# First batch of an FFT convolution, with the products laid out by (frequency of the pair, k2), ahead of a gated MLP in fp32 on one Trainium2 core

## The chip, the core and the metric

One core of one Trainium2 chip runs the whole program. The metric is the device time of one execution in microseconds (us), the median of several runs. A profiled execution has its own time, and its trace covers a span that is a little shorter than that time. The engines are named as in the profile: PE (TensorE, matmuls), PEld (its weight loads), DVE (VectorE), ACT (ScalarE), POOL (GpSimd) and SP (SyncE, which here only issues DMAs).

## What is computed

Two steps follow each other, all in fp32. The first is a long causal convolution, done by FFT, of `u = x * v` with a filter that a small MLP makes from `pos_emb`; its result is multiplied by `x`. The second is an MLP with a SiLU on 24,960 tokens.

```python
B, S, D = 2, 12480, 128
h_filt = (np.maximum(pos_emb @ w1, 0.0) @ w2) * np.exp(-0.01 * pos)[:, None]
Uf = np.fft.rfft(x * v, n=2 * S, axis=1)
Hf = np.fft.rfft(h_filt, n=2 * S, axis=0)
y = np.fft.irfft(Uf * Hf[None], n=2 * S, axis=1)[:, :S]
tok = (x * y).reshape(B * S, D)
h = tok @ moe_w_in                                # 128 -> 2048
out = (h / (1.0 + np.exp(-h))) @ moe_w_out        # 2048 -> 128
```

## The kernel before

The transform length is split as 2 x 98 x 64. The 98 outer frequencies are handled in 49 pairs (`NQ`), each of 2 outer frequencies `k` with 64 inner frequencies `k2`, real and imaginary parts `c` side by side. The program has three stages.

**Stage A** (to about 110 us) makes the filter's first transform `Xh` and the first transform `X` of batch 0.

**The products of batch 0** (about 110 to 284 us) are one loop, `for it in range(-1, NQ)`, with the steps of several pairs interleaved by hand. Every engine works through its own queue in the order in which the code issues. The steps are:

- `load_fb` loads a table `fb` of 256 KB for a pair, which holds its forward matrix (`[:, :, 0]`) and its inverse one (`[:, :, 1]`). It is issued on ACT's queue for pair `it + 4`; the buffers are seven deep.
- `pair_u` (L470, tile `up`): two matmuls of 128 x 128 with 256 columns give the pair's spectrum, with (c, k2) on the partitions. `times_i` (L487, L489, tile `uw`) copies it on ACT, halves of 64 partitions swapped and one negated.
- `hb_step` (L308, tile `hp`, copied to `zt` by ACT at L316): two matmuls of 128 x 128 with 128 columns, the filter's transform for pair `it + 3`.
- `spectrum` (L327, tile `sp`): 16 matmuls of 64 x 64 with 128 columns for pair `it + 1`. Eight of them are there because both halves of the partitions, c = 0 and c = 1, need the same filter values. Two ACT copies (L329) of 128 x 512 make `hab`, of which the lower 64 partitions are stored to `hs` for batch 1.
- `pair_p` (L495 and L502): `up` times `hab` on DVE (tile `at`), `uw` times `hab` on POOL (tile `bt`), each with one product of 512 and one of 256 elements per partition. `pair_s` (L508) adds `at` and `bt` on DVE, 768 elements, both in SBUF. `pair_v` (L512) adds the last 256 of them into the first part, on POOL (on DVE for the last two pairs).
- `last_w` for pair `it - 2`: `pair_w` (L470, tile `wp`, two buffers in two banks of PSUM), two matmuls of 128 x 128 with 256 columns, then `even_odd`: one ACT copy (L525), a sum and a difference on DVE (L527, L528), and two stores on SP's queue (L531) into `wd` in rows of 512 bytes, 64 partitions each. `ws` has two buffers.
- `side_steps` adds, from pair 25 on, loads of the MLP's weights, eight casts on ACT (L547), eight subtractions on DVE (L551, `wil`), loads of the second batch, and two products on POOL (L269, `spare`).

A string of letters, `seq3`, then orders what lies between this loop and the third stage; `s`, `v`, `u` and `U` in it stand for the sum, the last addition and the last two `last_w` of batch 0.

**The MLP** (from about 298 us to the end) runs over spans of 512 tokens, with the whole of batch 1's convolution threaded between its matmuls. `load_tile` (L647) reads `wd` back for `attn_tile` (L666). Batch 1 reads `hs` (`load_h`, L783) and `fb`, and uses `pair_p` and `even_odd` too.

PSUM has eight banks; the loop uses two each for `hp`, `sp`, `up` and `wp`.

Of the kernel before, what the change touches and what calls it, by code (L numbers as in the profile page):

```python
# [22 lines left out]
NB = 2  # L23
D = 128
# [41 lines left out]
def moe_tiles():  # L66
# [23 lines left out]
    seq3='smAvumULASahhllhhllaxxrrrrYLxhhllhhll',  # L90
# [4 lines left out]
def kernel(  # L95
# [16 lines left out]
    fb: bass.AP,  # L112
    win: bass.AP,
# [13 lines left out]
    hs = dram.tile([NQ, 64, 1024], F32, name="hs")  # L127
    wd = [dram.tile([2, NQ, 2, NI, C, D], F32, name=f"wd{b}") for b in range(NB)]
# [164 lines left out]
    def load_fb(rp, q, bufs, e):  # L293
        t = rp.tile([128, 2, 2, 128], F32, name=f"fb{q}", tag="fb", bufs=bufs)
        e.dma_start(out=t, in_=fb[q])
        return t
# [3 lines left out]
    def hb_step(q):  # L300

        if php is None:
            hp = psa.tile([128, 4, 256], F32, name=f"hp{q}", tag="ap", bufs=4)[:, 0]
            hp = hp.rearrange("p (k c n) -> p k c n", k=2, c=2)
        else:
            hp = php.tile([128, 2, 2, 64], F32, name=f"hp{q}", tag="hp", bufs=2)
        for k in range(2):
            nc.tensor.matmul(  # L308
                hp[:, k].rearrange("p c k -> p (c k)"),
                Xh[2 * q >= KA][:, 2 * q - (2 * q >= KA) * KA + k],  # L310
                fbs[q][:, k, 0],
                start=True,
                stop=True,
            )
        zs[q] = rpa.tile([128, 2, 2, 64], F32, name=f"zt{q}", tag="zt", bufs=3)
        nc.scalar.copy(out=zs[q], in_=hp)  # L316

    def spectrum(q, hab):

        zt = zs.pop(q)  # L320
        sp = [pps.tile([128, 2, 2, D], F32, name=f"sp{q}_{s}", tag=f"sp{s}", bufs=1) for s in range(2)]
        for k in range(2):
            for m in range(2):
                for s in range(2):
                    r = slice(64 * s, 64 * s + 64)
                    for h in range(0, 128, 64):
                        nc.tensor.matmul(sp[s][h : h + 64, m, k], zt[r, k, m], w2_sb[r], start=True, stop=True)  # L327
        for s in range(2):
            nc.scalar.copy(out=hab[:, :, s], in_=sp[s])  # L329
# [80 lines left out]
    for t in P["seq"]:  # L410
# [18 lines left out]
        elif t == "Z":  # L429
            begin(zq, zeros_block(n_z))  # L430
            n_z += 1
        elif t == "z":
            end(zq, False)
        elif t == "y":
            zw.append(zq[0])
            end(zq, True)
        elif t == "Y":
            end(zw)
        elif t == "H":
            begin(hq_, filter_group(n_h))  # L440
            n_h += 1
        elif t in "hg":
            end(hq_, t == "h")
        elif t in w_steps:
            next(w_steps[t], None)
        elif t == "|":
            early.release()
            xpool = pool("xpool")
            X = xpool.tile([128, R, NI * D], F32, name="X")
            rpa = pool("rp2a")  # L450
        elif t == "f":
            fbs[n_f] = load_fb(rpa, n_f, 7, nc.sync)
            n_f += 1
        elif t == "B":
            hb_step(len(zs))
# [36 lines left out]
    def pair_p(b, q, rp, u, hab, m, tag, nb, e):  # L492
# [5 lines left out]
            in1=hab[:, m, 0].unsqueeze(2).broadcast_to([128, 2, NI, D]),  # L498
# [4 lines left out]
            out=t[:, 2].rearrange("p (k d) -> p k d", k=2), in0=u[:, :, 0], in1=hab[:, m, 1], op=ALU.mult  # L503
# [17 lines left out]
    def even_odd(b, q, rp, wp, nb):  # L521

        p, tag, n = (rp, "ws", nb["ws"]) if b or q < NQ - 2 else (rpa, "fb", 7)
        ws = p.tile([128, 2, NI, D], F32, name=f"ws{b}_{q}", tag=tag, bufs=n)
        nc.scalar.copy(out=ws[:, 1], in_=wp[:, 1])  # L525
        yield ws
        nc.vector.tensor_tensor(out=ws[:, 0], in0=wp[:, 0], in1=ws[:, 1], op=ALU.add)  # L527
        nc.vector.tensor_tensor(out=ws[:, 1], in0=wp[:, 0], in1=ws[:, 1], op=ALU.subtract)  # L528
        yield ws
        for c in range(2):  # L530
            nc.sync.dma_start(  # L531
                out=wd[b][c, q].rearrange("e i t d -> t (e i) d"),
                in_=ws[64 * c : 64 * c + 64].rearrange("p e i d -> p (e i) d"),
            )
# [57 lines left out]
    nb = dict(up=2, uw=2, at=3, bt=2, wp=2, ws=2)  # L592

    def last_w(q):
        for _ in even_odd(0, q, rp, pair_w(0, q, pp, [(fbs.pop(q)[:, :, 1], prods.pop(q)[0])], nb), nb):
            pass

    for it in range(-1, NQ):
        if P.get("cut") and it == 4:
            for p in (rp, rpa, xpool, xha_pool, xhb_pool, const, pps, pp, php, dram):  # L600
                p.release()
            return
        if it + 4 < NQ:
            fbs[it + 4] = load_fb(rpa, it + 4, 7, nc.sync if it < 0 else nc.scalar)
        q = it
        if 0 <= q < NQ:
            up = pair_u(0, q, pp, [(fbs[q][:, :, 0], X[:, 2 * q : 2 * q + 2])], nb)
            _, uw = times_i(0, q, rp, up, nb)
        q = it - 1
        if 0 <= q < NQ:  # L610
            pair_s(*prods[q])
        q = it + 1
        if 0 <= q < NQ:
            hab = rp.tile([128, 2, 2, 2, D], F32, name=f"hab{q}", tag="hab", bufs=3)
            spectrum(q, hab)
            habs[q] = hab
        q = it + 3
        if 3 <= q < NQ:
            hb_step(q)
        q = it  # L620
        if 0 <= q < NQ:
            hab = habs.pop(q)
            _, at = pair_p(0, q, rp, up, hab, 0, "at", nb, nc.vector)
            _, bt = pair_p(0, q, rp, uw, hab, 1, "bt", nb, nc.gpsimd)
            prods[q] = at, bt
            nc.sync.dma_start(out=hs[q], in_=hab[0:64].rearrange("p m s k d -> p (m s k d)"))
        q = it - 1
        if 0 <= q < NQ:
            pair_v(prods[q][0], nc.vector if q >= NQ - 2 else nc.gpsimd)
        q = it - 2  # L630
        if 0 <= q < NQ:
            last_w(q)
# [10 lines left out]
    def load_tile(n):  # L643
        b, i, t2, m = tiles[n]
        w = sum(tile_widths(i, m))
        wt = slot(4096, 2 * 5 * D)[0:R].rearrange("p (c n) -> p c n", c=2)
        nc.sync.dma_start(  # L647
            out=wt[:, :, 0 : m * D],
            in_=wd[b][:, :, :, i, t2 : t2 + m].rearrange("c q e t d -> (c q) e (t d)"),
# [5 lines left out]
    def attn_tile(n, wt, xs, psp, tag):  # L655
# [5 lines left out]
        for t in range(m):  # L661
            for e in range(2):
                k = (ws[t] + 1 - e) // 2
                a = o + NQ * e
                for h in range(0, D, 64):
                    nc.tensor.matmul(  # L666
                        yp[h : h + 64, a : a + k],
                        wt[:, e, t * D + h : t * D + h + 64],
# [27 lines left out]
    for t in P["seq3"]:  # L696
# [7 lines left out]
        elif t == "s":  # L704
            pair_s(*prods[NQ - 1])
        elif t == "v":
            pair_v(prods[NQ - 1][0], nc.vector)
        elif t == "u":
            last_w(NQ - 2)
        elif t == "U":  # L710
            last_w(NQ - 1)
# [53 lines left out]
    def batch1_steps():  # L765
# [11 lines left out]
        def load_f(q):  # L777
            return load_fb(rp, q, 2, nc.sync)

        def load_h(q):  # L780
            hab = rp.tile([128, 2, 2, 2, D], F32, name=f"habr{q}", tag="hab", bufs=1)
            for h in range(2):
                nc.sync.dma_start(  # L783
                    out=hab[64 * h : 64 * h + 64].rearrange("p m s k d -> p (m s k d)"),
                    in_=hs[q],
# [179 lines left out]
def _constants():  # L965
# [14 lines left out]
    feo = np.stack([feo[:, 0::2], feo[:, 1::2]], axis=1)  # L980
    th = 2.0 * np.pi * ((k1[:, None, None] + 0.5) / N + k2[None, None, :] / C) * t2[None, :, None]
# [4 lines left out]
    fwd[1::2, C:] *= -1.0  # L986
    fb = np.stack([fwd, inv], axis=1).reshape(NQ, 2, 2, 128, 128).transpose(0, 3, 1, 2, 4)
# [4 lines left out]
    return {k: np.ascontiguousarray(a, dtype=np.float32) for k, a in dict(fa=fa, fs=fs, feo=feo, fe=fe, fb=fb, win=win).items()}  # L992
# [56 lines left out]
```

## Time and profile before

| | us |
|---|---|
| median of 3 runs | 1565.91 (1564.54 to 1567.79) |
| the profiled execution | 1563.66 |
| its span in the trace | 1561.9 |
| first product of batch 0 on DVE | at 113.13 |
| the same product of pair 48, the last one | at 278.94 |
| first matmul of the MLP | at 298.12 |

The profiled execution lies 2.25 us under the median, and the span 1.8 us under its execution. Over the whole span PE is busy 98%, DVE 80%, ACT 66% and POOL 41%; in the stretch of the products all four are busier than that, which the shares for the whole do not show.

To read the timeline below: each row has the start in us from the span's start, the duration in us, the engine, the line of the code, the operation, what it writes and reads, the shapes, and how many instructions were merged into the row. Brackets give the idle time of the engine just before it, and what ended it. A matmul in fp32 appears as two records, so "x4" is two matmuls. Ends of matmuls are modelled, and the start of the next row tells more than a row's duration.

### The profile page before, as it was taken

The page shows a single profiled execution, that of the slowest core. Times are in us where ns is not written, and L with a number is a line of the kernel's source. Part 1 is how long each engine was busy: PE and PEld are TensorE (multiplying, and loading weights), DVE is VectorE, ACT ScalarE, POOL GpSimd, SP SyncE. Part 2 cuts the span into 40 slices and gives each one's busy share as a digit, 9 for nine tenths or more (in the row PEclk, how much of TensorE's full clock was granted, in tenths as well). Part 3 has the DMA queues.
Part 4 walks back from the last instruction along what each step waited for, and adds up shares of the span by engine and source line. Part 5 has one row for each costly group of instructions (what it writes and reads, how often), then busy time and mean ns, then how long its engine had stood idle before and what let it go on. Part 6 is the DMA issues. An engine that isn't in the chain of part 4 may idle for free.

```text
span 1561.9 us, 32021 instructions
## 1 busy us (share of the span) xinstructions
PE 1529.9 (98%) x11928; PEld 1273.7 (82%) x11928; DVE 1242.8 (80%) x2091; ACT 1036.4 (66%) x1959; POOL 638.4 (41%) x669
## 2 busy tenths in 40 slices
PE   8989999799999999999999999999999999999999
PEld 8978877587788888888888888888888888888887
DVE  7558888667799999999999897777777777777776
ACT  2558887577777877877887775555555555555555
POOL 3658789422278887878788740000000000000000
PEclk9999999699999999999999999999999999999999
DMA  7667988745355555555555631111101211111100
GB/s 238 204 208 216 237 254 238 225 160 163 99 139 146 136 138 142 135 151 135 143 146 135 171 90 46 53 34 46 53 33 47 68 34 46 52 34 46 53 30 14
DMA packets 130612, 185.14 MB, mean 119 GB/s; under 512 B 12642, under 2 KB 75656, under 8 KB 130456
## 3 DMA queue, kind: packets, MB, share of 16 engines
q1 hardware_dynamic: 116120, 158.19, 37.1%
q10 hardware_dynamic: 14336, 24.90, 4.7%
q8 instruction: 94, 1.54, 0.4%
q14 instruction: 62, 0.51, 0.1%
HBM read 129.63 MB, written 53.41 MB: 117 GB/s over the span
## 4 chain that ended last, share of the span: by engine, by line
PE 89%; DVE 4%; DMA 3%; ACT 2%; issue 1%; POOL 1%; SPq 0%; ACTq 0%; DVEq 0%; POOLq 0%
PE op L939 12%; PE hq L906 11%; PE hq L907 11%; PE hq L908 11%; PE op L940 11%; PE op L941 11%; PE yp L666 4%; PE up L470 4%; PE wp L470 4%; PE sp L327 2%; PE aph L378 2%; PE ap L239 2%; PE ap L217 2%; PE hp L308 1%; DVE z L367 1%
## 5 line engine op out<-in xcount | busy, mean ns | idle before, releaser
L913 ACT ACTIVATE g<-hq 128x512 f32<-128x512 f32 x424 | 253.6, 598 | 265.4 <-PE hq L908 236.9
L918 DVE TENSOR_TENSOR gl<-g,gh 128x512 fp32r<-128x512 f32 x424 | 293.6, 692 | 94.4 <-PE hq L908 65.5
L939 PE MATMUL op<-gh,woh 128*128 128x512 f32 (+1 forms) x784 | 313.6, 400 | 0.0
L906 PE MATMUL hq<-ah,wih 128*128 128x512 f32 (+1 forms) x784 | 308.4, 393 | 2.2 <-ACT ah L688 1.4
L907 PE MATMUL hq<-al,wih 128*128 128x512 f32 (+1 forms) x784 | 306.1, 390 | 0.8 <-DVE al L690 0.8
L940 PE MATMUL op<-gl,woh 128*128 128x512 f32 (+1 forms) x784 | 305.9, 390 | 0.0
L908 PE MATMUL hq<-ah,wil 128*128 128x512 f32 (+1 forms) x784 | 305.7, 390 | 0.0
L941 PE MATMUL op<-gh,wol 128*128 128x512 f32 (+1 forms) x784 | 305.4, 390 | 0.0
L913 ACT ACTIVATE hq<-hq 128x512 f32<-128x512 f32 (+1 forms) x360 | 206.6, 577 | 89.3 <-PE hq L908 80.1
L918 DVE TENSOR_TENSOR gl<-hq,gh 128x512 fp32r<-128x512 f32 (+1 forms) x360 | 244.1, 683 | 23.2 <-ACT gh L917 14.3
L915 DVE CAST gh<-hq 128x512 fp32r<-128x512 f32 (+1 forms) x247 | 166.4, 674 | 41.9 <-ACT hq L913 41.4
L915 DVE CAST gh<-g 128x512 fp32r<-128x512 f32 x318 | 135.2, 425 | 72.0 <-ACT g L913 71.6
L906 PEld LDWEIGHTS hq<-ah,wih 128*128 128x128 f32 x784 | 148.0, 189 | 39.6 <-DVE gl L918 7.3
L908 PEld LDWEIGHTS hq<-ah,wil 128*128 128x128 f32 x784 | 148.1, 189 | 30.8
L907 PEld LDWEIGHTS hq<-al,wih 128*128 128x128 f32 x784 | 148.0, 189 | 30.5 <-DVE al L690 1.2
L941 PEld LDWEIGHTS op<-gh,wol 128*128 128x128 f32 x784 | 147.5, 188 | 30.8
L939 PEld LDWEIGHTS op<-gh,woh 128*128 128x128 f32 x784 | 147.7, 188 | 29.5 <-issue 0.2
L940 PEld LDWEIGHTS op<-gl,woh 128*128 128x128 f32 x784 | 148.1, 189 | 24.1 <-DVE gl L918 0.3
L495 POOL TENSOR_TENSOR bt<-uw,hab 128x512 f32<-128x512 f32 x49 | 74.1, 1513 | 29.6 <-ACT uw L489 29.6
L666 PEld LDWEIGHTS yp<-feo_sb,slots 98*64 98x64 f32 x2048 | 64.9, 140 | 22.9 <-issue 18.0
L666 PE MATMUL yp<-feo_sb,slots 98*64 98x49 f32 (+1 forms) x2048 | 71.5, 226 | 4.7 <-DMA slots<-wd 4.7
L269 POOL TENSOR_TENSOR slots<-slots 128x512 f32<-128x512 f32 x30 | 38.7, 1291 | 85.2 <-DMA slots<-in_ve_dram 81.9
(1066 smaller groups left out, 2543.6 us busy)
## 6 DMA issues: line engine op xcount, KB each, us to landing
slots<-hs SPq DMA_DIRECT2D x98, 256.0 KB
slots<-wd SPq DMA_DIRECT2D x48, 490.0 KB
hs<-hab SPq DMA_DIRECT2D x49, 256.0 KB
wd<-ws SPq DMA_DIRECT2D x98, 128.0 KB
slots<-in_fb_dram SPq DMA_DIRECT2D x49, 256.0 KB
wd<-slots SPq DMA_DIRECT2D x98, 128.0 KB
out_dram<-ot ACTq DMA_DIRECT2D x48, 256.0 KB
fb<-in_fb_dram ACTq DMA_DIRECT2D x45, 256.0 KB
```

The source lines that it names most:

```text
L470: nc.tensor.matmul(out[:, k].rearrange("p i d -> p (i d)"), f[:, k], a[:, k], start=(i == 0), stop=(i == len(passes) - 1),)
L495: e.tensor_tensor(out=t[:, 0:2].rearrange("p k (i d) -> p k i d", i=NI), in0=u, in1=hab[:, m, 0].unsqueeze(2).broadcast_to([128, 2, NI, D] ...
L666: nc.tensor.matmul(yp[h : h + 64, a : a + k], wt[:, e, t * D + h : t * D + h + 64], feo_sb[:, e, 0:k], start=True, stop=True,)
L906: nc.tensor.matmul(hp[:, 0:w], wih[:, fs], ah[:, 0:w], start=True, stop=False)
L907: nc.tensor.matmul(hp[:, 0:w], wih[:, fs], al[:, 0:w], start=False, stop=False)
L908: nc.tensor.matmul(hp[:, 0:w], wil[:, fs], ah[:, 0:w], start=False, stop=True)
L913: nc.scalar.activation(out=g[:, 0:w], in_=hp[:, 0:w], func=AF.Silu)
L915: nc.vector.tensor_copy(gh[:, 0:w], g[:, 0:w])
L918: nc.vector.tensor_tensor(out=gl[:, 0:w], in0=g[:, 0:w], in1=gh[:, 0:w].bitcast(F32), op=ALU.subtract)
L939: nc.tensor.matmul(o[:, 0:w], woh[:, fs], gh[:, 0:w], start=(f == 0), stop=False)
L940: nc.tensor.matmul(o[:, 0:w], woh[:, fs], gl[:, 0:w], start=False, stop=False)
L941: nc.tensor.matmul(o[:, 0:w], wol[:, fs], gh[:, 0:w], start=False, stop=(f == NF - 1))
```

## The change

The products of batch 0 get another layout. The partitions hold (k, k2), the pair's two outer frequencies, where they held (c, k2); c moves to the free dimension. With it:

- `u_step` makes the same `up` with four matmuls of 128 x 64 (the half of the partitions is that of k), and its two ACT copies are of all 128 partitions with 256 elements.
- `spectrum` has 8 matmuls in place of 16 and one ACT copy in place of two, since each filter value is now on one partition only. `hb_step` splits each matmul in two of 64 columns of weights. `hab` is half as large, and all of it goes to `hs`, as 128 rows of 2 KB where there were 64 of 4 KB.
- `a_early` and `a_late` take the place of `pair_p` on DVE: a product of 256 into SBUF, then the product of 512 back into `up` itself, in PSUM, and an addition of 256 there. `b_step` on POOL has the products of 512 and 256 and the addition of 256. `s_step` adds `up` and `bt`, 512 elements, into a new tile `ps`.
- `w_step` has four matmuls of 64 x 128 (rows of one k), accumulating over c. The two slots of its output lie in the halves of the same two banks (`wps`), and so do those of `sp` (`sps`). `even_odd`'s copy is issued with `w_step`; its DVE steps and its store, `ws_step`, one turn of the loop later.
- The order on PE is U, hp, sp, W, where it was U, sp, hp, W.
- W's results are stored by one DMA of 128 rows of 2 KB, in both batches; `load_tile` reads pieces of 1 KB where it read 2.5 KB.
- Batch 0 has tables of its own, `fb0`, loaded six pairs ahead into nine buffers.

```diff
+        for c in range(2):
+            for k in range(2):
+                nc.tensor.matmul(
+                    up[64 * k : 64 * k + 64, c].rearrange("p i d -> p (i d)"),
+                    fbs[q][:, k, 0, 64 * c : 64 * c + 64],
+                    X[:, 2 * q + k],
+                    start=True,
+                    stop=True,
+                )
...
+        nc.scalar.activation(out=uw[:, 0], in_=up[:, 1], func=AF.Copy, scale=-1.0)
+        nc.scalar.copy(out=uw[:, 1], in_=up[:, 0])
...
+    def a_early(q, up, hab):
...
+        times_h(nc.vector, a2, up[:, :, 0], hab[:, 0, 1])
+    def a_late(up, hab, a2):
+        times_h(nc.vector, flat(up), flat(up), hab[:, 0, 0])
+        add(nc.vector, up[:, :, 1], up[:, :, 1], a2)
...
+    def b_step(q, uw, hab):
...
+        times_h(nc.gpsimd, flat(b01), flat(uw), hab[:, 1, 0])
+        times_h(nc.gpsimd, bt[:, 2], uw[:, :, 0], hab[:, 1, 1])
+        add(nc.gpsimd, b01[:, :, 1], b01[:, :, 1], bt[:, 2])
...
+    def s_step(q):
...
+        add(nc.vector, prods[q].rearrange("p c (i d) -> p c i d", i=NI), up, bt)
+    def w_step(q):
+        wp = wps[:, :, q % 2]
+        for c in range(2):
+            for k in range(2):
+                r = slice(64 * k, 64 * k + 64)
+                nc.tensor.matmul(wp[:, k], f[r, c, 1], p[r, c], start=(c == 0), stop=(c == 1))
+        wss[q] = even_odd(0, q, rp, wp.rearrange("p k (i d) -> p k i d", i=NI), nb)
+        next(wss[q])
...
     for it in range(-1, NQ):
-        if it + 4 < NQ:
-            fbs[it + 4] = load_fb(rpa, it + 4, 7, nc.sync if it < 0 else nc.scalar)
+        while n_f <= min(it + 6, NQ - 1):
+            fbs[n_f] = load_fb(fb0, rp, n_f, 9, nc.sync if it < 0 else nc.scalar)
+            n_f += 1
...
-        for c in range(2):
-            nc.sync.dma_start(
-                out=wd[b][c, q].rearrange("e i t d -> t (e i) d"),
-                in_=ws[64 * c : 64 * c + 64].rearrange("p e i d -> p (e i) d"),
-            )
+        nc.sync.dma_start(
+            out=wd[b][q].rearrange("c t i e d -> (c t) (i e d)"), in_=ws.rearrange("p i e d -> p (i e d)")
+        )
```

In a turn `it` of the new loop the order is: load, U(it), `ws_step`(it - 3), `a_early`(it), `s_step`(it - 1), `hb_step`(it + 3), `spectrum`(it + 1), `a_late`(it), `b_step`(it), store to `hs`, W(it - 2), `side_steps`. In `seq3` the letter `v` falls away.

## Rows read from the trace of the kernel before

**Rows 1.** Windows: length, each engine's busy time, granted clock, DMA share, GB/s.

```profile
160.00:200.00 40.00, 40.00 (x525) 32.16 (x523) 33.67 (x60) 32.77 (x72) 31.77 (x36) 1.00 0.90 232
240.00:280.00 40.00, 36.70 (x453) 28.68 (x454) 35.05 (x58) 30.07 (x64) 37.22 (x36) 1.00 0.87 232
...
500.00:700.00 200.00, 199.41 (x1206) 165.58 (x1205) 186.72 (x305) 158.16 (x313) 161.84 (x179) 1.00 0.56 143
```

**Rows 2.** Timeline of PE over one turn of the products' loop.

```profile
161.49 1.10 PE L327 MATMUL sp<-w_sb,zt 64*64 64x128 f32 x32
...
162.53 0.71 PE L308 MATMUL hp<-fb,Xha 128*128 128x128 f32 x4
...
163.08 1.03 PE L470 MATMUL wp<-at,fb 128*128 128x256 f32 x4
...
163.94 1.03 PE L470 MATMUL up<-X,fb 128*128 128x256 f32 x4
...
164.90 0.34 PE L327 MATMUL sp<-w_sb,zt 64*64 64x128 f32 x4
```

**Rows 3.** Timeline of DVE over the same turn.

```profile
161.15 0.42 DVE L527 TENSOR_TENSOR ws<-wp,ws 128x256 f32<-128x256 f32 x1 [0.55 <-ACT ws L525]
...
161.61 0.42 DVE L528 TENSOR_TENSOR ws<-wp,ws 128x256 f32<-128x256 f32 x1
...
161.95 1.12 DVE L508 TENSOR_TENSOR at<-at,bt 128x768 f32<-128x768 f32 x1
...
163.00 0.68 DVE L495 TENSOR_TENSOR at<-up,hab 128x512 f32<-128x512 f32 x1
...
163.59 0.41 DVE L502 TENSOR_TENSOR at<-up,hab 128x256 f32<-128x256 f32 x1
```

**Rows 4.** Timeline of POOL, ACT and SP's queue over the same turn.

```profile
162.06 1.24 SPq L531 DMA_DIRECT2D wd<-ws  x2
...
163.01 1.28 POOL L495 TENSOR_TENSOR bt<-uw,hab 128x512 f32<-128x512 f32 x1 [0.76 <-ACT uw L489]
...
164.14 0.38 ACT L525 COPY ws<-wp 128x256 f32<-128x256 f32 x1
...
164.24 0.73 POOL L502 TENSOR_TENSOR bt<-uw,hab 128x256 f32<-128x256 f32 x1
...
164.92 0.74 POOL L512 TENSOR_TENSOR at<-at 128x256 f32<-128x256 f32 x1
```

**Rows 5.** Timeline of PE where matmuls use half the array's columns, or rows.

```profile
63.03 7.21 PE L217 MATMUL ap<-fa_sb,xs 98*64 98x98 f32 x166 [1.00 <-ACT X L228]
...
311.37 1.14 PE L239 MATMUL ap<-fe_sb,slots 49*128 49x98 f32 x16
```

**Rows 6.** Timeline at the loop's start, ACT and DVE.

```profile
112.47 0.58 ACT L489 COPY uw<-up 64x512 f32<-64x512 f32 x1
...
113.13 0.69 DVE L495 TENSOR_TENSOR at<-up,hab 128x512 f32<-128x512 f32 x1 [3.81 <-DMA fb<-in_fb_dram]
```

**Rows 7.** Timeline: the same DVE product of pairs 28, 37 and 48.

```profile
207.26 0.68 DVE L495 TENSOR_TENSOR at<-up,hab 128x512 f32<-128x512 f32 x1
...
239.66 0.68 DVE L495 TENSOR_TENSOR at<-up,hab 128x512 f32<-128x512 f32 x1
...
278.94 0.68 DVE L495 TENSOR_TENSOR at<-up,hab 128x512 f32<-128x512 f32 x1
```

**Rows 8.** Timeline: side work on DVE and POOL, and what ran beside it.

```profile
213.02 0.84 DVE L551 TENSOR_TENSOR wil<-spare,wih 128x256 fp32r<-128x256 f32 x1
...
259.12 1.26 POOL L269 TENSOR_TENSOR spare<-spare 128x512 f32<-128x512 f32 x1
...
259.23 1.97 DVE L508 TENSOR_TENSOR at<-at,bt 128x768 f32<-128x768 f32 x1
```

**Rows 9.** Timeline: two stores of one pair, and a copy that waits for a store.

```profile
252.64 1.25 SPq L531 DMA_DIRECT2D wd<-ws  x2
...
258.03 0.37 ACT L525 COPY ws<-wp 128x256 f32<-128x256 f32 x1 [0.22 <-DMA wd<-ws]
```

More of the change, by code (lines that the diff above doesn't have):

```diff
@@ L126 @@
     dram = dpool("dram")
-    hs = dram.tile([NQ, 64, 1024], F32, name="hs")
-    wd = [dram.tile([2, NQ, 2, NI, C, D], F32, name=f"wd{b}") for b in range(NB)]
+    hs = dram.tile([NQ, 128, 512], F32, name="hs")
+    wd = [dram.tile([NQ, 2, C, NI, 2, D], F32, name=f"wd{b}") for b in range(NB)]
     const = pool("const")
@@ L307, in hb_step @@
         for k in range(2):
[L308 to L313, printed above, removed]
-            )
+            for s in range(2):
+                r = slice(64 * s, 64 * s + 64)
+                nc.tensor.matmul(
+                    hp[r, k].rearrange("p c k -> p (c k)"),
+                    Xh[2 * q >= KA][:, 2 * q - (2 * q >= KA) * KA + k, r],
+                    fbs[q][:, k, 0],
+                    start=True,
+                    stop=True,
+                )
         zs[q] = rpa.tile([128, 2, 2, 64], F32, name=f"zt{q}", tag="zt", bufs=3)
@@ L320, in spectrum @@
         zt = zs.pop(q)
[L321 to L329, printed above, removed]
+        sp = sps[:, :, q % 2]
+        for m in range(2):
+            for s in range(2):
+                r = slice(64 * s, 64 * s + 64)
+                for k in range(2):
+                    nc.tensor.matmul(sp[64 * k : 64 * k + 64, s, m], zt[r, k, m], w2_sb[r], start=True, stop=True)
+        nc.scalar.copy(out=hab.rearrange("p m s d -> p s m d"), in_=sp)
     nc.vector.memset(w1_sb, 0.0)
@@ L502, in pair_p @@
         e.tensor_tensor(
-            out=t[:, 2].rearrange("p (k d) -> p k d", k=2), in0=u[:, :, 0], in1=hab[:, m, 1], op=ALU.mult
+            out=t[:, 2].rearrange("p (k d) -> p k d", k=2), in0=u[:, :, 0], in1=hab[:, :, m, 1], op=ALU.mult
         )
@@ new lines, in times_h, with flat, add @@
+    def times_h(e, out, u, h):
+        e.tensor_tensor(out=out, in0=u, in1=h.unsqueeze(1).broadcast_to([128, u.shape[1], D]), op=ALU.mult)
+    def flat(t):
+        return t.rearrange("p c i d -> p (c i) d")
+    def add(e, out, a, b):
+        e.tensor_tensor(out=out, in0=a, in1=b, op=ALU.add)
+    def a_early(q, up, hab):
+        a2 = rp.tile([128, 2, D], F32, name=f"at{q}", tag="at", bufs=nb["at"])
+        times_h(nc.vector, a2, up[:, :, 0], hab[:, 0, 1])
+        return a2
+    def a_late(up, hab, a2):
+        times_h(nc.vector, flat(up), flat(up), hab[:, 0, 0])
+        add(nc.vector, up[:, :, 1], up[:, :, 1], a2)
@@ L596, in last_w, with ws_step @@
+    def w_step(q):
+        p, f = prods.pop(q), fbs.pop(q)
+        wp = wps[:, :, q % 2]
+        for c in range(2):
+            for k in range(2):
+                r = slice(64 * k, 64 * k + 64)
+                nc.tensor.matmul(wp[:, k], f[r, c, 1], p[r, c], start=(c == 0), stop=(c == 1))
+        wss[q] = even_odd(0, q, rp, wp.rearrange("p k (i d) -> p k i d", i=NI), nb)
+        next(wss[q])
+    def ws_step(q):
+        for _ in wss.pop(q):
             pass
+    wss = {}
     for it in range(-1, NQ):
[L599 to L602, printed above, removed]
@@ L609 @@
+        q = it
+        if 0 <= q < NQ:
+            a2 = a_early(q, up, habs[q])
         q = it - 1
         if 0 <= q < NQ:
[L611 to L616, printed above, removed]
+            s_step(q)
         q = it + 3
@@ L619 @@
             hb_step(q)
+        q = it + 1
+        if 0 <= q < NQ:
+            hab = rp.tile([128, 2, 2, D], F32, name=f"hab{q}", tag="hab", bufs=3)
+            spectrum(q, hab)
+            habs[q] = hab
         q = it
@@ L622 @@
             hab = habs.pop(q)
[L623 to L629, printed above, removed]
+            a_late(up, hab, a2)
+            prods[q] = up, b_step(q, uw, hab)
+            nc.sync.dma_start(out=hs[q], in_=hab.rearrange("p m s d -> p (m s d)"))
         q = it - 2
         if 0 <= q < NQ:
-            last_w(q)
+            w_step(q)
         side_steps(it)
```

78 lines of the change are left out of this document (49 added, 29 removed).

## The prediction

> **What bounds the kernel now.** I read the windows first, then one turn of the products' loop on PE, then the other engines over the same turn, and last how long the turns are. The windows [rows 1] say where the change can count. From 500 to 700 us PE is busy 199.41 of 200 us at full clock with DMA at 0.56, and the MLP's matmuls stay as they are, so what the change does there (stores in one piece, reads in pieces of 1 KB) can only matter if it makes PE wait, and a DMA share of 0.56 leaves room. The loop of the products has PE at 40.00 of 40 too, but DVE, ACT and POOL are at 80 to 84% and DMA at 0.90: four resources close to full, and the gain ends at the second one.
>
> On PE one turn goes from sp at 161.49 to the next sp at 164.90, 3.41 us, with no idle time in it [rows 2]: sp 1.04 (start to start), hp 0.55, wp 0.86, up 0.96. DVE in that turn waits 0.55 for a copy of W, so it has about 2.85 us of work [rows 3]; POOL has 1.28 + 0.73 + 0.74 = 2.75 and waits 0.76 [rows 4]. So PE sets the turn. The whole loop: DVE's first product runs from 113.13 for pair 0 to 207.26 for pair 28, 94.1 us or 3.36 a turn; then 32.4 us for nine turns with side work on DVE; then 39.3 us for eleven turns up to 278.94 [rows 6, 7].
>
> **PE, term by term.** Between wp and up nothing changes but the data, so 0.86 us is the plain price of two matmuls of 256 columns, 0.43 each [rows 2]. By that price hp's two of 128 columns are 0.43 and took 0.55; up is 0.86 and took 0.96; sp's sixteen quarter-size matmuls, four abreast, are 0.86 and took 1.04. The excess, 0.12 + 0.10 + 0.18 = 0.40, lies where the shape of the tile changes, which it does twice in a turn (up to sp, sp to hp): 0.20 a change.
>
> New turn. U: four matmuls of half the columns, two abreast, 0.86 if they run abreast. The row of Stage A says they do [rows 5]: 83 matmuls (166 records) of 98 columns in 7.21 us, 0.087 each, where the plain price of 98 columns is 0.165 and half of it 0.082. hp in halves: 0.43. sp: eight, 0.43. W: four matmuls of half the rows, 0.86 if abreast. The nearest row is L239, eight matmuls of 98 columns in at most 1.14 us [rows 5], 0.14 each, up to 1.73 times the abreast price; but its row ends with the emptying of the pipe, and each of its matmuls has few columns for its 128 columns of weights. I take 0.86, because sp has two halves of the rows at work at once and came out at the abreast price; the upper end is 0.86 x 1.73 = 1.49. Sum of streams 2.58. The changes of shape become three (hp to sp, sp to W, W to U; U and hp share one), 0.60. **PE: 3.18 a turn**, 0.23 less than now, with ends at 2.58 + 0 and 3.81.
>
> The Trainium skill, TensorEngine Tiling (Array Packing), section Key Properties, says that a change of tiling mode, unlike a change of tile, drains the engine, which speaks against a turn with three modes in place of two. The trace agrees, with the 0.40 us above; the page gives no price, and without the rule the new turn on PE would be 2.58.
>
> **DVE.** Starts to starts [rows 3]: 0.46 and 0.34 for the two steps of ws, 1.05 for the 768-element addition, 0.59 for a product of 512; 0.41 is the product of 256. New: ws 0.80, `a_early` 0.34 to 0.41, `s_step` 0.59 (512 elements, one operand in PSUM), then `a_late`, which writes to PSUM. No row has DVE writing there. I take the same product into SBUF, 0.68, plus 0.04 since the next step needs its result (L528 starts 0.04 after the end of L527, whose result it reads), and 0.42 for the addition. Below this it could be the start-to-start prices, 0.59 + 0.34; above, I bound it by the slowest same-size row, the addition that took 1.97 for 768 [rows 8], 1.31 for 512 and 0.66 for 256. DVE is 2.87 a turn, between 2.7 and 3.7. That slowest row has another use: it ran beside a POOL product [rows 8], and the 768-element addition, the one DVE step with both operands in SBUF, is gone.
>
> **POOL** keeps 2.75, as the last addition moves onto `bt` [rows 4]. **ACT** loses a copy of 512 elements and half of the two uw copies' length: five copies of 256 or 512 elements, under 2.3 us at 0.38 for 256 [rows 4]. **Queues.** SP issues one W store a pair where it issued two (1.24 us for two [rows 4]); the store now stands ahead of the one to `hs` in a turn, which waits for nothing. ACT issues one table load a turn as before. Bytes are unchanged, about 768 KB a pair; at 3.18 us that is 247 GB/s against 232 at a share of 0.90 [rows 1], so I expect DMA nearly full but not the bound.
>
> **New waits.** (a) `up` is held longer: U of pair n + 2 needs `s_step` of pair n. The ring is U 0.96, two ACT copies 0.76, `a_early` 0.41, `s_step` 0.68 and four hand-overs of some 0.07: 3.09, of which one passes per turn. It stays under 3.18 by little. I have DVE wait for both ACT copies because at the loop's start it began 0.08 us after the second one ended, having idled 3.81 [rows 6]; the row names a DMA, so this is likely, not certain. Queued behind that DVE wait are `s_step` and `a_late`, and PE's next U behind them. (b) `ws` has two buffers and its store goes out a turn later: 1.7 us from the copy's start to the store's issue (copy 0.38, DVE's `a_late` to its end about 0.4, ws 0.80, hand-overs), landing L, for two pairs: (1.7 + L) / 2 a turn. In [rows 9] the copy at 258.03 waits for a store two pairs back, issued from 252.64: L is up to 5.4 there, which gives 3.55; at 4.6 or less it costs nothing. Queued behind that ACT wait are the next pair's copies. (c) At the end W of pair 48 can't overwrite banks that pair 47's DVE steps still read: 0 to 1.0 us, I take 1.0 (W's 0.86 and two hand-overs).
>
> The Trainium skill, PSUM — Partial Sum Buffer, section on PSUM bank collisions, has two engines on one bank and the same partitions collide, so software must order them, readers too. By it (a) and (c) are real waits; without it the tail's 1.0 falls away and the sum below is 1.0 us better.
>
> **Sum.** 28 turns: 94.1 - 28 x 3.18 = 5.1 us. Nine turns, eight of them with a subtraction on DVE of at most 0.84 [rows 8], at least the 0.41 of its size: 2.87 + 0.53 = 3.40, so 8 x 3.40 + 3.18 = 30.4, gain 2.0. Eleven turns: 35.0, plus two POOL products of 1.26 [rows 8] against a spare of 0.43 a turn and about 0.7 before `s_step` needs `bt`, some 1.0, plus 1.0 for waits on stores: gain 2.3. Tail -1.0. Start 0: the first U still waits for Stage A's last copies; tables for three pairs go out at once there, 0.5 either way. MLP 0: its cover is PE's queue of matmuls between a tile's load and its use; the first tile's 490 KB alone stands open, same bytes, 0.5 either way. Total 8.4 us: the profiled 1563.66 becomes 1555.3, the median 1565.91 becomes 1557.5.
>
> **Rivals.**
> - Changes of shape cost less, or overlap: the turn falls to the ring of (a), about 3.0. For: 0.20 is a mean of unlike halves. Against: all three load new weights behind a drain. 40 turns at 0.18 less: 1550.
> - DVE takes over: writing to PSUM is dear, or DVE and POOL still disturb each other, and the turn stays at 3.3 to 3.4. For: no row shows such a write. 1563 to 1566, no change.
> - Slower by the store's ring (b): with L over 5.1 us through the loop the turn is over 3.41. At 5.4 it is 3.55, 0.14 x 49 more: 1572. For: the wait is in the trace already, 0.22 us. Against: one such wait in a stretch with loads of the second batch beside it; one store of the same bytes takes the place of two issued one behind the other.
> - Slower because W's halves of the rows run only partly abreast: from 1.27 times 0.86 on the turn passes 3.41; at 1.73 times it is 3.81: 1584.
>
> **How the numbers follow.** Forecast (1553 to 1562) 0.55; cheaper changes 0.20; DVE 0.13; store's ring 0.07; W's halves 0.05. A measurement of this kernel tells about 0.2%, 3.1 us, from no change. Faster by more: 0.55 + 0.20 + 0.02 of the DVE case = 0.77; within: 0.11; slower: 0.12. The range 1549 to 1567 takes in the first three cases and leaves out the two slower ones and the best end of the second.
>
> **What would show it.** In the new profile: starts of U, hp, sp and W on PE 0.86 to 1.1, 0.5 to 0.6, 0.5 to 0.7 and about 1.0 apart, and a turn near 3.2; hab copied once per pair; POOL's product of 512 near 1.28 in every turn; `a_late` at 0.68 and 0.42. I am wrong if PE waits for DVE's `s_step` in the first 28 turns, if W's step is over 1.2, or if ACT's copy of W often waits for a store.

## The result, and the profile after

| | before | after |
|---|---|---|
| median of 4 runs each, us | 1565.22 (1564.08 to 1567.79) | 1546.32 (1545.19 to 1548.27) |
| ratio | | 0.9878, 95% interval 0.9861 to 0.9895 |
| the profiled execution, us | 1563.66 | 1546.87 |
| its span, us | 1561.9 | 1545.0 |

The change saves 18.9 us by the medians, and 16.9 us between the two traces. The forecast was 8.4 us (1557.5), and 1546.3 lies under the low end of the range, 1549. The direction was right and the size was under half.

The traces are cut at the same events: the first matmul of U for pairs 0, 28, 37 and 48, the last DVE step of `ws`, the first matmul of `yp` (the MLP's first tile, which needs the read-back of `wd`), and the first matmul `hq` of the MLP.

| stretch | before, us | after, us | gain | forecast gain |
|---|---|---|---|---|
| start to U(0) | 110.62 | 110.54 | 0.1 | 0 |
| U(0) to U(28), 28 turns | 94.18 | 86.42 | 7.8 | 5.1 |
| U(28) to U(37), nine turns with side work | 31.83 | 28.38 | 3.5 | 2.0 |
| U(37) to U(48), eleven turns | 39.28 | 35.17 | 4.1 | 2.3 |
| U(48) to the last DVE step of `ws` | 8.78 | 10.43 | -1.7 | -1.0 |
| from there to `yp` | 9.61 | 6.75 | 2.9 | 0 |
| `yp` to `hq`, and the MLP to the end | 1267.57 | 1267.32 | 0.2 | 0 |

So 6.0 of the 8.5 us that the forecast lacks lie in the loop, and 2.9 in the stretch behind it, less 0.7 at the loop's end.

One turn of PE in the kernel after, to be held against [rows 2] (columns as there):

```profile
162.72 1.08 PE L602 MATMUL up<-X,fb 128*64 128x256 f32 x8
163.64 0.61 PE L311 MATMUL hp<-fb,Xha 128*64 128x128 f32 x8
164.17 0.67 PE L329 MATMUL sps<-w_sb,zt 64*64 64x128 f32 x16
164.77 1.13 PE L652 MATMUL wps<-ps,fb 64*128 64x256 f32 x8
165.84 0.44 PE L602 MATMUL up<-X,fb 128*64 128x256 f32 x2
```

Start to start, U takes 0.92 us, hp 0.53, sp 0.60 and W 1.07: the turn is 3.12 (3.11 over many turns), where it was 3.41. No idle time stands in brackets.

The same turn on DVE, beside [rows 3]:

```profile
162.44 0.69 DVE L615 TENSOR_TENSOR up<-up,hab 128x512 f32<-128x512 f32 x1
163.16 0.43 DVE L621 TENSOR_TENSOR up<-up,at 128x256 f32<-128x256 f32 x1
163.51 0.41 DVE L529 TENSOR_TENSOR ws<-wps,ws 128x256 f32<-128x256 f32 x1
163.95 0.42 DVE L530 TENSOR_TENSOR ws<-wps,ws 128x256 f32<-128x256 f32 x1
164.62 0.42 DVE L615 TENSOR_TENSOR at<-up,hab 128x256 f32<-128x256 f32 x1 [0.24 <-ACT uw L611]
164.96 0.68 DVE L621 TENSOR_TENSOR ps<-up,bt 128x512 f32<-128x512 f32 x1
```

DVE idles 0.24 us a turn and waits, as forecast, for the second ACT copy of U. The product that writes to PSUM takes 0.69 us and its addition 0.43: no dearer than the same into SBUF (0.68 and 0.41 to 0.42 [rows 3]).

The groups of POOL's instructions from 160 to 200 us show the other side (busy time and mean ns of one behind the bar, then idle time):

```profile
L615 POOL TENSOR_TENSOR bt<-uw,hab 128x512 f32<-128x512 f32 x13 | 16.6, 1274 | 4.5 <-ACT uw L611 4.5
L615 POOL TENSOR_TENSOR bt<-uw,hab 128x256 f32<-128x256 f32 x13 | 9.5, 733 | 0.0
L621 POOL TENSOR_TENSOR bt<-bt 128x256 f32<-128x256 f32 x13 | 9.5, 729 | 1.0
```

And of the kernel before, DVE's 768-element addition in the same stretch:

```profile
L508 DVE TENSOR_TENSOR at<-at,bt 128x768 f32<-128x768 f32 x12 | 14.2, 1180 | 0.0
```

Its mean is 1.18 us where the shortest of the loop took 0.95: it was longer, beside POOL, in most turns, not only at the one row of [rows 8].

The windows of the kernel after, beside [rows 1]:

```profile
160.00:200.00 40.00, 40.00 (x520) 27.04 (x516) 36.03 (x79) 24.51 (x66) 34.53 (x39) 1.00 0.78 260
500.00:700.00 200.00, 199.77 (x1209) 165.89 (x1208) 187.44 (x305) 159.72 (x314) 163.05 (x180) 1.00 0.49 142
```

PE is still at 40.00 of 40, DVE rose from 33.67 to 36.03, ACT fell from 32.77 to 24.51, and DMA moves more (260 against 232 GB/s) with less of its time (0.78 against 0.90).

### The profile page after: what moved, and what is told of

Same layout as the page of the kernel before. It is cut to its first block, busy times and chain, and to the rows that moved or that the text cites. A ratio compares the mean times of both kernels' runs of the same rounds, so it can differ in the third digit from the quotient of the medians.

```text
span 1545.0 us, 31519 instructions
## 1 busy us (share of the span) xinstructions
PE 1514.3 (98%) x11732; PEld 1245.1 (81%) x11732; DVE 1227.3 (79%) x2138; ACT 990.2 (64%) x1910; POOL 633.5 (41%) x671
## 3 DMA queue, kind: packets, MB, share of 16 engines
q8 instruction: 93, 1.52, 0.4%
## 4 chain that ended last, share of the span: by engine, by line
PE 91%; DVE 3%; DMA 2%; ACT 1%; issue 1%; POOL 1%; ACTq 0%; SPq 0%; DVEq 0%; POOLq 0%
PE op L1001 12%; PE hq L968 11%; PE hq L969 11%; PE op L1002 11%; PE hq L970 11%; PE op L1003 11%; PE yp L727 4%; PE wps L652 3%; PE up L602 3%; PE ap L218 2%; PE wp L471 2%; PE aph L379 2%; PE ap L240 2%; PE up L471 2%; PE sps L329 2%; PE hp L311 1%
## 5 line engine op out<-in xcount | busy, mean ns | idle before, releaser
L970 PEld LDWEIGHTS hq<-ah,wil 128*128 128x128 f32 x784 | 148.0, 189 | 31.1
L969 PEld LDWEIGHTS hq<-al,wih 128*128 128x128 f32 x784 | 148.0, 189 | 30.3 <-DVE al L751 1.1
L615 POOL TENSOR_TENSOR bt<-uw,hab 128x512 f32<-128x512 f32 x98 | 96.2, 1004 | 17.8 <-ACT uw L611 17.5
```

Source lines behind the costliest of these rows:

```text
L615: e.tensor_tensor(out=out, in0=u, in1=h.unsqueeze(1).broadcast_to([128, u.shape[1], D]), op=ALU.mult)
L969: nc.tensor.matmul(hp[:, 0:w], wih[:, fs], al[:, 0:w], start=False, stop=False)
L970: nc.tensor.matmul(hp[:, 0:w], wil[:, fs], ah[:, 0:w], start=False, stop=True)
```

## The experiments

Each ratio below is to the kernel before, in runs on the same chip. The kernel after has 0.9878 (0.9861 to 0.9895); 0.002 is 3.1 us. The lengths of turns and of stretches are taken from one trace of each kernel, by the starts of U.

### What bounds the turn: the matmuls of sp issued twice

```diff
 def spectrum(q, hab):
-        for m in range(2):
+        for m in range(4):
+            m = m // 2
```

> The changed kernel, but each of the eight matmuls of the spectrum is issued twice in a row with the same operands, so that its result is the same and TensorE has 0.43 us more to stream in every turn of the pair loop. Theory (the turn is bound by TensorE's four groups of matmuls, with the ring of `up` at 3.05 just under it): the turn goes from 3.11 to 3.54, less the 0.05 that the ring allows nothing for, so 3.5; 49 turns by 0.4 is about 20 us more, 1566, ratio near 1.000. Rival (a ring of waits through VectorE or ScalarE sets the turn and TensorE stands idle in it): the matmuls fit into idle time, and the time rises by less than 8 us.

Measured: 0.9985 (0.9971 to 0.9998), 1563.81 us.

```profile
166.72 0.61 PE L311 MATMUL hp<-fb,Xha 128*64 128x128 f32 x8
167.26 1.10 PE L330 MATMUL sps<-w_sb,zt 64*64 64x128 f32 x32
168.29 1.13 PE L653 MATMUL wps<-ps,fb 64*128 64x256 f32 x8
169.35 1.08 PE L603 MATMUL up<-X,fb 128*64 128x256 f32 x8
170.27 0.61 PE L311 MATMUL hp<-fb,Xha 128*64 128x128 f32 x8
```

The timeline of PE: sp grew from 0.60 to 1.03, by 0.43, and the turn from 3.11 to 3.55. It is 3.55 in every turn from the third up to the last but two, those with side work too, and from 125 to 280 us PE waits for nothing. The loop's 48 turns take 167.9 us against 150.0 in the kernel after, near the 20 us that were expected. So in the kernel after PE sets the turn, and the rival, in which PE has idle time in it, falls. The 0.43 is the plain price of matmuls of a quarter of the array, four abreast. That those of half the columns and of half the rows stream at the plain price too is read from the trace of the kernel after: the records of U's and of W's matmuls start in pairs 0.007 us apart, and from the second pair on a pair starts every 0.216 us, as the single records of `up` do in the kernel before.

### What a change of shape costs: sp ahead of hp

The old order of the two on PE, in the new layout. A turn then has four changes of shape in place of three (U to sp, sp to hp, hp to W, W to U).

```diff
-        hb_step(it + 3)
         spectrum(it + 1)
+        hb_step(it + 3)
```

> The changed kernel with sp issued ahead of hp, as before the change: the shapes of a turn are then 128x64, 64x64, 128x64, 64x128, four changes in place of three, with the same matmuls. Theory PE: one change of shape more costs about 0.18 us, turn 3.11 to 3.29, 49 turns: 8 to 9 us slower than the changed kernel. Theory stores, or any in which PE has slack: under 2 us.

Measured: 0.9903 (0.988 to 0.9926), 1550.26 us.

```profile
164.33 1.08 PE L602 MATMUL up<-X,fb 128*64 128x256 f32 x8
165.34 0.67 PE L329 MATMUL sps<-w_sb,zt 64*64 64x128 f32 x16
165.94 0.66 PE L311 MATMUL hp<-fb,Xha 128*64 128x128 f32 x8
166.53 1.14 PE L652 MATMUL wps<-ps,fb 64*128 64x256 f32 x8
167.59 1.08 PE L602 MATMUL up<-X,fb 128*64 128x256 f32 x8
```

The turn is 3.26, 0.15 more. The time is in U, 1.01 for 0.92 now that another shape follows it, and in hp, 0.59 for 0.53 now that W follows it instead of sp. One change of shape costs 0.15 us here, and the order that the change gave to hp and sp is worth 0.15 x 28 = 4.2 of its 7.8 us in the first stretch (the traces: 90.35 against 86.42, 3.9). All 48 turns take 155.6 us against 150.0, 5.6 more where 8 to 9 were expected, since the turns with side work were over 3.11 already. By the totals alone, 3.9 us apart, the two orders are not told apart.

### One change of shape fewer: W in quarters

W's four matmuls of 64 x 128 become eight of 64 x 64, the shape of sp, so that two changes are left.

```diff
-                nc.tensor.matmul(wp[:, k], f[r, c, 1], p[r, c], ...)
+                for h in range(0, 128, 64):
+                    nc.tensor.matmul(wp[h : h + 64, k], f[r, c, 1, h : h + 64], p[r, c], ...)
```

> The changed kernel with W's four matmuls of 64x128 made eight of 64x64, four abreast: same streams (0.86), but sp and W then have one shape, and a turn has two changes of shape. Theory PE with the ring of up close behind it (s_step of a pair must end before U of the pair after next starts; the turns without hp at the loop's end run at 3.05 and show that ring): the turn falls from 3.11 to 3.05, 3 us faster than the changed kernel. Theory PE alone, ring looser than 2.93: 2.93, 9 us faster.

Measured: 0.9848 (0.9829 to 0.9867), 1542.23 us.

```profile
166.09 0.67 PE L329 MATMUL sps<-w_sb,zt 64*64 64x128 f32 x16
166.58 1.04 PE L653 MATMUL wps<-ps,fb 64*64 64x256 f32 x16
167.69 1.08 PE L602 MATMUL up<-X,fb 128*64 128x256 f32 x8
168.57 0.64 PE L311 MATMUL hp<-fb,Xha 128*64 128x128 f32 x8
169.14 0.67 PE L329 MATMUL sps<-w_sb,zt 64*64 64x128 f32 x16
```

The turn goes to 3.05, as the first theory had it, and not to 3.11 - 0.15 = 2.96; the 48 turns take 148.0 us against 150.0. W now follows sp without a change, but the next U starts 1.11 us after W's start. To see what holds it, the next run shortens the ring of `up`.

### The ring of `up`: s_step ahead of a_early, alone and with W in quarters

DVE adds up pair `it - 1` before it starts on pair `it`, so `up` comes free one step of DVE earlier.

```diff
-            a2 = a_early(it, up, habs[it])
             s_step(it - 1)
+            a2 = a_early(it, up, habs[it])
```

> The changed kernel with s_step of the pair before issued on DVE ahead of a_early, which waits for U and two ACT copies. That loosens the ring of up by about 0.4 us and nothing else. Theory PE: no change (within 1 us), the turn stays at 3.11, since PE sets it and not the ring.

> Both: W in quarters and s_step first. Theory PE with ring: with the ring loose the turn falls to PE's new sum, 2.93 (two changes of shape), or to DVE's and POOL's 2.8, whichever is more: 2.93 x 49, some 8 to 9 us faster than the changed kernel, and a further 5 us faster than W in quarters alone. If W in quarters alone already gives the 9 us, the ring was never close.

Measured: alone 0.9878 (0.9856 to 0.99), 1547.38 us; with W in quarters 0.9847 (0.9826 to 0.9868), 1542.09 us. Alone the turn stays at 3.11 in the first 28, since PE sets it; but the nine turns with side work take 30.45 us where they took 28.38, which the expectation did not have. With W in quarters the turn falls, from the third on, to between 2.91 and 3.15, on average 2.98, and the first 28 turns to 82.94 us, from 84.83. So 3.05 was the ring of `up`, the wait (a) of the prediction, put there at 3.09. What makes some of the turns longer than 2.91 was not looked into. The total is 4 to 5 us under the kernel after, where 8 to 9 were expected, and no lower than with W in quarters alone, because here too the nine turns rose, from 28.29 to 30.79. Two rows of DVE in those turns, and POOL beside the second:

```profile
209.60 0.41 DVE L551 TENSOR_TENSOR wil<-spare,wih 128x256 fp32r<-128x256 f32 x1
...
212.84 0.89 DVE L551 TENSOR_TENSOR wil<-spare,wih 128x256 fp32r<-128x256 f32 x1
```

```profile
212.72 0.73 POOL L621 TENSOR_TENSOR bt<-bt 128x256 f32<-128x256 f32 x1
```

In the new order every second subtraction on DVE starts just behind POOL's addition, which runs on for 0.61 us beside it, and takes 0.48 us longer. W then waits 0.58 us for `ws`, and the turn is 3.72 instead of 3.25.

In the kernel after the two meet as well, but there the subtraction starts 0.08 us ahead, and it is POOL's addition that grows, to 0.93 from 0.73, on an engine with time to spare:

```profile
216.61 0.41 DVE L551 TENSOR_TENSOR wil<-spare,wih 128x256 fp32r<-128x256 f32 x1
```

```profile
216.69 0.93 POOL L621 TENSOR_TENSOR bt<-bt 128x256 f32<-128x256 f32 x1
```

### Both, with the old order in the turns with side work

> W's product in four matmuls of half-width and half-height, and s_step ahead of a_early as in the run with both, except in the turns of pairs 27 to 37, which carry the side work and where the order of the changed kernel is kept. Theory (in the turns with side work VectorE's subtraction and a_early set the turn, so the early order is better there; elsewhere the ring of `up` does): turns of 2.91 to 2.95 outside, U0 to U28 82.9 and 37 to 48 34.5 as with both, and 28.3 for the nine turns instead of 30.8; so about 2.5 us below the run with both, ratio near 0.983. Rival (the order in those turns is not what made them longer, the shorter turns before are): the nine turns stay at 30.8 and the time at that of the run with both, 0.985.

Measured: 0.9834 (0.9811 to 0.9858), 1540.78 us.

```profile
L551 DVE TENSOR_TENSOR wil<-spare,wih x8: 415/415/416, 196.7 to 218.7; 128x256 fp32r<-128x256 f32 x8
```

The eight subtractions (shortest, median, longest in ns) are all at 0.415, and the nine turns take 28.21 us; elsewhere the turn is as in the run with both, 82.96 us for the first 28. The rival falls: the nine turns are short again behind short turns, and in the run with s_step first alone they were long behind turns of 3.11. This is the fastest kernel of the study, 0.0044 of the ratio or 6.9 us under the kernel after. By intervals it isn't told apart from the two runs with W in quarters before it; in the traces 2.6 us stand in the nine turns, where they were looked for. The expectation named a longer DVE turn as the cause; the rows show the collision with POOL instead, and who starts first in it.

### What keeps DVE and POOL apart: a_late into SBUF

In the kernel after, `s_step` reads one operand from PSUM, since `a_late` writes back into `up`. Here it writes into a tile `as` in SBUF, so that `s_step` and the addition of `a_late` have both operands there. For room the tables are loaded four ahead into seven buffers; the run on the tables' depth, below, has them four ahead too, in nine buffers, and is the nearest control.

```diff
-        times_h(nc.vector, flat(up), flat(up), hab[:, 0, 0])
-        add(nc.vector, up[:, :, 1], up[:, :, 1], a2)
+        times_h(nc.vector, flat(a0), flat(up), hab[:, 0, 0])
+        add(nc.vector, a0[:, :, 1], a0[:, :, 1], a2)
```

> The changed kernel with a_late writing its product to a tile in SBUF, so that its addition and s_step's have both operands in SBUF, as the old 768-element addition had; tables four ahead and seven buffers, to make room. Theory collision (a DVE step with two SBUF operands and a POOL step hold each other up, as the 1.47 and 1.99 us beside each other in the kernel before): POOL's product of 512, 1.27 in every turn of the changed kernel, grows again towards 2, and the turn goes to 3.25 to 3.5: 7 to 18 us slower than the changed kernel. Theory PE alone: POOL and DVE have 0.3 and 0.2 us to spare a turn, the turn stays under 3.15, within 2 us.

Measured: 0.9999 (0.9984 to 1.0014), 1566.98 us. The whole gain is gone.

```profile
130.55 0.41 DVE L615 TENSOR_TENSOR at<-up,hab 128x256 f32<-128x256 f32 x1
130.88 1.32 DVE L621 TENSOR_TENSOR ps<-as,bt 128x512 f32<-128x512 f32 x1
132.13 0.68 DVE L615 TENSOR_TENSOR as<-up,hab 128x512 f32<-128x512 f32 x1
132.84 0.42 DVE L621 TENSOR_TENSOR as<-as,at 128x256 f32<-128x256 f32 x1
```

```profile
130.39 2.41 POOL L615 TENSOR_TENSOR bt<-uw,hab 128x512 f32<-128x512 f32 x2
132.88 0.98 POOL L621 TENSOR_TENSOR bt<-bt 128x256 f32<-128x256 f32 x1
```

`s_step` takes 1.32 us where it took 0.68. POOL's two products take 2.41 where they took 1.27 + 0.73 = 2.00, and its addition 0.98 for 0.73. The product of 512, which the expectation had growing, stays at 1.27; the one of 256 behind it grows, to 1.18 in most turns. Neither engine has idle time left, and PE waits 0.24 us a turn for `ws`: the turn is 3.43. The loop's 48 turns take 171.0 us against 150.0; 48 x 0.32 is 15.4 of these 21.0, and the rest lies in single turns of 3.7 to 5.1. Part of that rest goes with the depth of the tables: the run below, four ahead without the change to `a_late`, takes 154.3, and against it the loop is 16.7 us longer. (The trace is of an execution of 1572.65 us, 5.7 over this median; its first U starts 4.8 us later than in the kernel after.) The rows fit a take-turns rule: POOL's product, begun at 130.39, would end after 1.27 us at 131.66, and the addition of 0.68 that came to DVE meanwhile would then end at 132.34; it ends at 132.20. The Trainium skill, SBUF — State Buffer, section "SBUF: two separate sides", says so: VectorE with two inputs in SBUF and GpSimd reading SBUF share a pair of ports as an exclusive lock, held for the whole instruction. The trace agrees, and the two DVE products, with one operand in PSUM, take 0.41 and 0.68 beside POOL as ever.

### The tables: four ahead in place of six

```diff
-        while n_f <= min(it + 6, NQ - 1):
+        while n_f <= min(it + 4, NQ - 1):
```

> The changed kernel with the tables loaded four pairs ahead where it has six (buffers unchanged). Theory PE: no PE wait for a table at a turn of 3.11, since hp needs a table one turn after its load is issued and a load landed in 3 to 5 us in the kernel before; with the order on PE now U before hp the margin is small, so 0 to 3 us slower. Theory tables (depth carries part of the gain): 5 us or more slower, with PE waiting for loads in most turns.

Measured: 0.9879 (0.9852 to 0.9906), 1546.94 us. The total shows nothing of the depth, within some 4 us to either side. The trace shows a part of it: from 113 to 262 us PE waits for tables (us in total, times, longest), for which the kernel after has no row:

```profile
PE hp L311 <- DMA fb<-in_fb_dram: 2.3, 6, 0.7
```

The 48 turns take 154.3 us against 150.0, and in this one trace the stretches ahead of the loop and behind it are shorter by nearly as much. So theory PE holds in kind, the prediction's nothing is not refuted, and what the depth is worth, between nothing and some 4 us, stays open.

### The stores: undone, and alone

Two runs: the kernel after with `ws`, `wd` and the read-back as before (two stores a pair, rows of 512 bytes, read back in pieces of 2.5 KB), and the kernel before with only the new ones (one store, rows of 2 KB, pieces of 1 KB). No run parts the number of stores, the rows and the pieces.

```diff
-        nc.sync.dma_start(out=wd[b][q]..., in_=ws...)
+        for c in range(2):
+            nc.sync.dma_start(out=wd[b][c, q]..., in_=ws[64 * c : 64 * c + 64]...)
```

> The changed kernel with W's results stored as before (two DMAs a pair, rows of 512 bytes, both batches) and read back in pieces of 2.5 KB. Theory PE (the turn of the products is PE's sum of streams and changes of shape, 3.11 us, and nothing else binds): the turn stays at 3.11 to 3.15 and the loop loses at most 2 us; what comes back is only in the transition to the MLP, up to 2.9 us, where the last store and the first read-back lie on the path. So 0 to 4 us slower than the changed kernel. Theory stores (a good part of the gain of 18.9 us is that rows of 2 KB took DMA from a share of 0.90 to 0.78): the turn goes to 3.2 or more, and the kernel is 7 us slower or more.

> The kernel before with only the new stores and the read-back in pieces of 1 KB. Theory PE: its turn stays at 3.36 on average, since PE was full there; only the transition gets up to 2.9 us shorter: 0 to 4 us faster than before. Theory stores: 7 us or more faster than before.

Measured: undone 0.9907 (0.9883 to 0.993), 1550.61 us; alone 0.9942 (0.9925 to 0.996), 1558.09 us. So the stores are worth 0.0029 x 1566 = 4.5 us in the kernel after (whose interval reaches about 0 to 9 us) and 9 us (6 to 12) in the kernel before. They were put at 0. Undone, they cost more in the loop than the 2 us that theory PE allowed and less in all than the 7 of theory stores; alone, the total is what theory stores named, though the turn stays at 3.41, as theory PE had it.

Where it goes is in the traces. With the new layout and the old stores, ACT waits in the loop, from 113 to 260 us (us in total, times, longest):

```profile
ACT ws L527 <- PE wps L654: 15.4, 30, 0.7
ACT ws L527 <- DMA wd<-ws: 10.3, 10, 1.7
```

That is the wait (b) of the prediction, ten times up to 1.7 us. In the kernel after there is no row for it. The window of 160 to 200 us, to be held against 0.78 and 260 GB/s in the kernel after:

```profile
160.00:200.00 40.00, 40.00 (x518) 27.00 (x516) 36.05 (x78) 24.79 (x67) 34.58 (x39) 1.00 0.95 262
```

The 48 turns take 153.4 us with the old stores and 150.0 with the new ones: 3.4 us. Behind the loop, from the last DVE step of `ws` to `yp`, it is 8.70 against 6.75.

In the kernel before, where PE set the turn at 3.41, the new stores give only 0.7 us in the loop. The timelines of SP's queue and PE of the kernel before with the new stores:

```profile
285.64 0.34 SPq L646 DMA_DIRECT2D slots<-wd  x1
```

```profile
289.62 2.37 PE L665 MATMUL yp<-feo_sb,slots 98*64 98x49 f32 x40 [3.47 <-DMA slots<-wd]
293.43 0.69 PE L905 MATMUL hq<-ah,wih 128*128 128x384 f32 x1 [1.43 <-ACT ah L687]
```

And of the kernel before:

```profile
289.21 0.95 SPq L647 DMA_DIRECT2D slots<-wd  x1
```

```profile
294.30 2.38 PE L666 MATMUL yp<-feo_sb,slots 98*64 98x49 f32 x40 [4.70 <-DMA slots<-wd]
```

And of the kernel after:

```profile
277.69 2.38 PE L727 MATMUL yp<-feo_sb,slots 98*64 98x49 f32 x40 [2.78 <-DMA slots<-wd]
```

From the last DVE step of `ws` to `yp` it is 9.61 us before (last store issued 1.52 after that step, read-back 3.00 later, `yp` 5.09 later) and 7.03 with the new stores alone: the second store of the last pair is gone, and both the store and the read-back land sooner. The spans of these two traces differ by 6.0 us: 0.7 in the loop, 2.6 here, and 2.7 in Stage A and the MLP together. The last part is not settled, and so it is open why the totals differ by 9 us and the traces by 6.0: Stage A, whose code is the same in every kernel here but for its table loads and the filter's first steps, ended between 108.4 and 115.4 us in the traces of this study.

## Why the prediction came out too small

The mechanism held: PE sets the turn of the loop, before and after. What failed are the sizes of terms in the sum. Of the 8.5 us that the forecast lacks between the traces, 2.9 are the step "MLP 0", put at nothing because the bytes stay the same; 2.6 are the price of a change of shape in PE's turn (1.8 in the first stretch, 0.8 in the eleven turns); 1.5 are the nine turns, priced by a subtraction that was in a collision; 1.0 are waits on stores that did not come, and 0.9 the first two turns. Against these the tail was 0.7 longer; 0.3 lie ahead of the loop and in the MLP.

**PE's turn, the main term, was right in kind and 0.07 too long.** PE sets the turn (shown by sp issued twice), matmuls of half the rows and of half the columns run abreast (W 1.07, U 0.92 start to start), and the number of changes is three. The term that was mis-sized is the price of a change: 0.20, worked out as a mean over two changes of the old turn. The streams sum to 2.58, so three changes cost 3.11 - 2.58 = 0.53, or 0.18 each. They are not equal: a fourth costs 0.15, and without the one from sp to W the shortest turns are 0.20 below. Over 26 of the 28 turns that is 1.8 us. Another 0.9 us is the first two turns, which have no W and took 2.05 and 3.45, together 5.50, where 28 x 3.18 counted 6.36. The rival "changes of shape cost less" came nearest, 1550, but by a turn near 3.0, which neither PE (3.11) nor the ring of `up` (3.05) reached.

**The rule on drains.** The prediction weighed the Trainium skill, TensorEngine Tiling (Array Packing), Key Properties: a change of mode drains the engine, against 2.58 without it. The turns of 3.26, 3.11 and 2.91 with four, three and two changes agree with it (the last is the shortest turn with `s_step` first, so that the ring of `up` does not hide it).

**DVE's turn held, side work did not.** DVE was put at 2.87 and is 2.87 (3.11 less 0.24). The nine turns were put at 2.87 + 0.53 = 3.40 with the subtraction at up to 0.84 [rows 8]. In the kernel after it takes 0.41 in all eight, 0.33 start to start, and the turns alternate between 3.20 and 3.12. The prediction had seen half of this: it read that the lengthened addition of [rows 8] ran beside POOL and was gone after the change, but called that addition the one DVE step with both operands in SBUF, and the subtraction is another. So it took the 0.84 as part of its price, though that row is the same collision: POOL's addition at L512 ran from 212.85 for 0.72 us beside it. The nine turns were forecast at 30.4 and took 28.4. Of these 2.0 us 1.5 count as gain, since the starts of U put the old stretch at 31.8, where DVE's product had it at 32.4.

**Eleven turns.** The two products on POOL cost 0.21 and 0.85 us (turns of 3.32 and 3.96), 1.06 where 1.0 was put. The 1.0 us for waits on stores did not come, and 11 turns at 0.07 are 0.8: together the 1.8 us that were missing.

**Stores in the loop.** The wait (b) is real, as the old stores in the new layout show; the rival of 1572 took L as [rows 9] show it, and with the new stores no such wait is left. The prediction priced a store by its bytes, which didn't change; the number of stores and the length of their rows did.

**MLP 0, "the first tile's 490 KB alone stands open, same bytes, 0.5 either way".** This step failed by 2.9 us, outside its own bounds. [Rows 9] showed a store's landing, but no row of the stretch between the last `ws` and `yp` was read, where nothing hides a transfer: PE waits there 4.70 us for the read-back, and 2.78 in the kernel after. With the old stores in the new layout the stretch is 2.0 us longer, with the new ones in the old layout 2.6 shorter, so most of the 2.9 is the stores.

**Tail.** W(48) does wait for pair 47's DVE steps, 1.47 us where 1.0 was put:

```profile
265.42 1.13 PE L652 MATMUL wps<-ps,fb 64*128 64x256 f32 x8 [1.04 <-DVE ws L530]
268.02 2.02 PE L652 MATMUL wps<-ps,fb 64*128 64x256 f32 x8 [1.47 <-DVE ws L530]
```

No run leaves this order out, so none tests the rule on banks that the prediction gave for it. The last W takes 2.02 instead of 1.13 in a stretch, from 268.1 to 271.5, in which the granted clock was 0.50, its lower level of 1.2 GHz; PE had stood idle for 1.04 and 1.47 us before it fell, as the two rows show. In the other traces with the new layout in which the clock was still at 2.4 GHz there, this stretch takes 9.5 to 9.6 us, 0.8 more than before.

**Not tried:** `ws` with three buffers, the number of stores apart from the length of their rows, and the MLP's own share of the stores.

## What to carry to other kernels

Between two phases there is a stretch in which the first tile of the next phase waits for the last store of the one before: read it in the trace on its own, since a transfer that is hidden everywhere else stands bare there. When an engine's instruction shows two durations for one shape, find the partner that it collides with before taking either as its price, and see if one of its operands can stay in PSUM. Where PE is the bound, count how often the shape of its tile changes in a turn, order the groups so that equal shapes meet, and then look for the ring of waits just under the new turn.

## What the runs showed of the hardware

- A change of tile shape on PE cost 0.15 to 0.20 us in a turn of fp32 matmuls: four changes a turn took 3.26 us, three 3.11 and two 2.91 at the shortest.
- A product of DVE that writes back into PSUM took 0.69 us for 512 elements, against 0.68 into SBUF, and kept clear of POOL: a DVE addition with both operands in SBUF, beside POOL, took 1.32 instead of 0.68, and POOL's instructions grew too.
- Where a DVE subtraction with both operands in SBUF met a POOL addition, the one that started second grew: DVE's from 0.41 to 0.89 us when it came 0.12 us behind, POOL's from 0.73 to 0.93 when it came 0.08 behind.
- Two DMA issues of one pair's result took 0.6 us each on SP's queue and one for the same bytes 0.32. In the new layout the DMA share was 0.95 at 262 GB/s with two stores a pair in rows of 512 bytes, and 0.78 at 260 GB/s with one in rows of 2 KB.
